# Sliding-window attention beside a dense layer: block 0's queries from raw x, exponentials summed by halving adds, and a new order of the pieces

## The chip, the cores and the metric

The kernel runs on one core of a Trainium2 chip. The metric is the device time of one execution in microseconds (us). The engines run side by side and meet by semaphores: TensorE (PE: matrix products, with its weight loads PEld), VectorE (DVE), ScalarE (ACT), GpSimd (POOL) and SyncE (SP), which issues most of the DMA transfers. The median of the three runs shown is 209.95 us (209.86 to 210.22).

## The reference

x has 2048 rows of 640 in bf16. It is normalized row by row; the normalized rows go through two layers side by side, and both results are added to x:

```python
xn = layernorm(x)                       # (x - mean) / sqrt(var + 1e-5)
# A: 32 heads of 20; each row looks at itself and at 7 rows, 2 apart, before it
q, k, v = split(xn @ wqkv)
logits = einsum("bhsd,bhswd->bhsw", q, kg) * 20 ** -0.5   # kg: the 8 rows of k
attn = softmax(where(mask, logits, -1e9))
A = einsum("bhsw,bhswd->bhsd", attn, vg) @ wo
# B: dense, 1536 wide
B = gelu(xn @ w1 + b1) @ w2 + b2
out = x + A + B
```

## The kernel before, in words

**Tiles.** The rows come in four chunks (n = 0 to 3) of 512, each of four blocks of 128. A normalized block is turned, so that the 640 columns lie on partitions in five tiles of 128 (xnT). Chunk 0's blocks are turned by TensorE (do_tp, L274) and copied out of PSUM (do_tc, L282); the other chunks by DMA (do_td, L290). From xnT come q, k and v (do_pj, L331, evicted by do_pc, L397) and the dense layer's hidden tiles (do_f1, L595, with the gelu in do_ge, L607). VectorE multiplies q by the shifted k (do_qk, L428), adds some of the five column tiles (do_pa L461, do_pb L467), and TensorE sums over each head (do_lg, L472). Then comes the softmax over eight positions (do_max, do_sub, do_exp, do_sum, do_recip, do_attn, L507 to L549), the weights are spread over the partitions by DMA (expand, L560), VectorE multiplies them by v and adds (do_av L575, do_add L585, do_ot L589) to oT, and TensorE forms the result from the hidden tiles and oT: turned for chunks 0 to 2 (do_t, L663, the DMAs do_ut and do_ud), straight for chunk 3 (do_o, L620).

**Order.** Nothing is scheduled by the compiler: ORDER (L41 to L71) lists some 700 pieces by name, and each engine runs its instructions in the order in which the pieces are listed. A name tells the piece, the chunk and the part: `f10_5` is do_f1 of chunk 0 and tile 5, `lg2` is do_lg of chunk 2, `t004` is the part of do_t for chunk 0 and column tile 0 that multiplies oT. An instruction that must wait holds back all that is listed behind it on its engine. The same holds for SP's transfers. PSUM has four buffers for products (psA), two for turned blocks and results (psO) and one for scores (psL).

**The start.** SP loads block 0 of x, ScalarE's queue block 1; then SP loads q's weights in one transfer, k's, blocks 2 and 3, v's, and so on (L134 to L146). TensorE runs 13 products of ones (do_warm, L443) so that it is not idle at first. Block 0's mean and variance come from VectorE (do_st, L206), block 1's from ScalarE by sums (do_su L220, do_sq L227, do_mean1 L236). do_rs (L241) makes the reciprocal deviation, do_xn (L259) normalizes, and q of blocks 0 and 1 is formed 128 columns at a time as xnT grows (do_ga, do_gd, L347 to L373). From then on, chunk 0's q, k and v are formed for two blocks at once (do_gp, L375, evicted by do_gq, L388).

**The sums.** do_sum (L528) adds the eight exponentials of each head and row in one reduction on VectorE, read with the positions innermost, into a small f32 tile. do_recip (L534) takes its logarithm and exponential on ScalarE. Chunk 0's softmax runs in two halves (PARTS, L34).

Of the kernel before, what the change touches and what calls it, by code (L numbers as in the profile page):

```python
# [32 lines left out]
TURNED = 4  # L33
PARTS = (2, 1, 1, 1)  # L34
# [7 lines left out]
pad01 pad02 st00a st00 sum1 rs00 mean1 neg1 sq1 xn00a xn00b tp00a wa tp00b wb tc00a tc00b rs01 ga xn01a xn01b gb2  # L42
tp01a gb3 tp01b tc01a tc01b gb4 gd gc0 ge tb b1 hj102 gc1 ho st02a st02 st03a hc102 gc4 st03 hj101 rs02 xn02 rs03 xn03
st10a st12a st13a st11a hc101 st12 hj100 hc100 hj200 tp02 tc02 tp03 tc03 pk st13 hj201 hc200 st11 st10 hj202 hc202
hj012 hc012 hc201 rs1 rc1 hj112 hc112 xn12 tc12 xn10 hj210 qk000 hj011 hc011 tc10 hj110 hc110 qk001 hj010 hc010 hc210
hj111 hc111 qk011 qk010 pa011 pa001 xn11 tc11 xn13 hj211 hc211 f10_5 tc13 f10_4 ge0_4 ge0_5 f10_0 ge0_0 f10_7 f10_10
pj113 pc113 pj103 pj111 ge0_10 pj101 pc111 pj114 ldx ge0_7 pa000 pc101 pa010 lg0 mask m0a ld2 pc103 pj102 pc114 pad11
su21 mx0a ex0a pj112 pc112 m0b mx0b ss0a pc102 ex0b ri0a ss0b pj100 pc100 at0a ri0b at0b pj110 pj104 pc104 pc110 xd0
qk111 f10_2 ge0_2 su22 qk100 hj212 hc212 f10_6 ge0_6 pj121 su20 f10_1 pc121 su23 ldo f11_10 ge1_10 ng2 ge0_1 sq20
f11_5 f10_11 pj122 pc122 f10_3 qk110 sq22 t040 qk101 f11_0 t000 lg1 xp0 av010 ge0_3 sq21 xs0 ge1_0 sq23 rs2 f10_8  # L50
ge0_8 t001 m1 f11_3 rc2 xn23 tc23 ge0_11 av031 t041 mx1 av021 xn20 tc20 f11_7 av011 ge1_5 ge1_7 av001 ge1_3 xp1 f10_9
t042 t002 xn21 ge0_9 tc21 pj120 xn22 tc22 av030 av000 f11_9 ge1_9 pj124 ex1 av020 ss1 pc120 pc124 pj123 pc123 ad00 ri1
t043 f11_2 t003 pj204 at1 pc204 xd1 su31 ad01 pad12 ad02 ot0 pj200 pc200 pj201 pc201 av101 xp2 pj212 su30 pc212 pj220
pj213 pc220 pc213 pj223 pc223 pj211 su33 pc211 pj203 su32 ng3 sq33 pad21 av100 sq31 pj202 f11_6 t004 u00 av110 xs1
av130 t044 av120 av131 av121 t010 av111 t011 t012 t013 u04 t020 t014 sq32 pc203 pc202 pj221 sq30 rs3 rc3 ad11 u01 ut00
ad10 ad12 t030 pj210 pc221 t031 t021 t022 ut01 ge1_2 pj214 xn33 tc33 t032 t033 t034 xn31 tc31 ge1_6 pj224 t023 t024
f11_8 ot1 pc214 pad22 pc210 qk201 qk211 qk210 xn30 tc30 f12_9 qk200 f11_1 pa210 pa201 xn32 ge1_8 u02 pa211 pa200 f11_4
ge1_1 t100 ge1_4 tc32 pj311 pc311 pb212 ud00 ud01 ge2_9 pj310 pc310 pad31 pj304 pc304 pj314 pc314 t101 pj300 pj324
pc324 ut02 pj303 f12_10 pb202 pc224 u03 pc303 xp3 pj301 pc301 xl ge2_10 pc300 f13_9 pj313 pc313 pj312 ud02 ut03 ud03
pj302 pc302 f13_6 ge3_6 pj323 lg2 pc312 qk300 m2 pc323 f11_11 ge1_11 f13_0 ge3_0 mx2 ut04 f13_11 ge3_9 ex2 pa300 ss2  # L60
qk310 ri2 at2 xs2 qk301 t130 t131 f12_1 ge2_1 ge3_11 t132 f13_10 qk311 t102 t103 f13_2 pa310 xd2 t104 pj320 pc320
f13_1 ge3_1 u10 ut10 ud10 f12_8 pa311 pa301 pb312 ge2_8 f13_8 ge3_8 t110 t133 t111 t112 t113 t114 u11 ge3_10 f12_5
pj222 pc222 pj321 pc321 pb302 lg3 av200 t134 u13 m3 av221 ge2_5 xb3 f12_11 t140 t141 t120 ut11 mx3 f12_2 ge3_2 av211
ex3 ss3 ri3 av220 ge2_2 f13_5 ge2_11 t142 t143 t121 t122 t123 f12_6 ge2_6 at3 xs3 f12_3 ge2_3 t124 u12 f12_7 pj322
ud04 av210 av201 av231 f12_0 t144 ge2_7 ge2_0 t200 av230 pc322 u14 ut12 ud11 f12_4 ge2_4 ge3_5 f13_4 ge3_4 o310 f13_7
ge3_7 t210 ad20 ad21 ad22 ot2 f13_3 t201 t202 pad32 av321 t203 ge3_3 o311 av331 ut13 av320 xd3 t204 u20 av300 ut14
ut20 ud12 ud13 t211 t212 t240 t213 t214 av311 u21 ud20 t241 t242 av310 av330 t220 t221 t222 t223 t224 u22 ut21 t243
av301 ad30 ad31 o330 o331 t230 ad32 t231 t232 t233 t234 u23 ut22 ud21 t244 u24 o312 ut23 o313 ud22 ud23 ot3 o320 o321
o322 o323 o324 oc32 od32 ut24 o314 oc31 od31 o300 o301 o302 o303 o304 o332 o333 o334 ud14 ohi ud24 oc30 od30 oclo ochi
ochd  # L70
# [4 lines left out]
def kernel(  # L75
# [63 lines left out]
    load_w(0)  # L139
    load_w(1)  # L140
    load_x(2, BPC)
    load_w(2)
# [21 lines left out]
    make_identity(nc, ident[:])  # L164
    eps_t = consts.tile([P, 1], F32, name="eps_t")
# [70 lines left out]
    def do_mean1():  # L236
        nc.vector.tensor_scalar(
            out=mv[:, 1, 0:1], in0=col(acc, 0, 1), scalar1=1.0 / D, scalar2=None, op0=ALU.mult
        )

    def do_rs(n, b0, b1):  # L241
        sl = slice(n * BPC + b0, n * BPC + b1)
        summed = n in ACT_STATS or (n, b0) == (0, 1)
        table(LOG_SET)
        nc.scalar.activation(
            logv[:, sl], mv[:, sl, 1], ACT.Ln, bias=eps_t[:], scale=1.0 / D if summed else 1.0
        )
        nc.scalar.activation(rstd[:, sl], logv[:, sl], ACT.Exp, scale=-0.5)
# [95 lines left out]
    def bank(key):  # L344
        return get(("bank", key), lambda: psA.tile([P, BPC, P], F32, tag="acc", name="gps"))

    def q_piece(bl, to, ti, first, last):  # L347
        ps, slot = (bank(bl), to) if to < BPC else (bank(BPC), bl)
        nc.tensor.matmul(  # L349
            ps[:, slot, :],  # L350
            lhsT=wqkv_p[0][:, ti, to, :],
            rhs=tiles["xnT", 0][:, ti, bl * P : (bl + 1) * P],
            start=first,
            stop=last,
            skip_group_check=True,
        )

    def do_ga(a, b):
        for ti in range(a, b):
            for to in range(KT):  # L360
                q_piece(0, to, ti, ti == 0 and to in (0, BPC), ti == KT - 1 and to == BPC - 1)

    def do_gd(a, b):
        for ti in range(a, b):
            for to in range(KT):
                q_piece(1, to, ti, ti == 0 and to == 0, ti == KT - 1 and to >= BPC - 1)

    def do_gc(g):
        q = pair_of(0, 0)
        if g == BPC:  # L370
            nc.scalar.copy(q[:, BPC, 0 : 2 * P].rearrange("p (b m) -> p b m", b=2), bank(BPC)[:, 0:2, :])
        else:
            nc.scalar.copy(q[:, 0:BPC, g * P : (g + 1) * P], bank(g)[:])  # L373

    def do_gp(which, pair, a, b):  # L375
        ps = psA.tile([P, 2, 2 * P], F32, tag="acc", name="gps")
        tiles["pair", which, pair, a] = ps
        for to in range(a, b):
            for ti in range(KT):
                nc.tensor.matmul(  # L380
                    ps[:, to - a, :],
                    lhsT=wqkv_p[which][:, ti, to, :],
                    rhs=tiles["xnT", 0][:, ti, pair * 2 * P : (pair + 1) * 2 * P],
                    start=(ti == 0),
                    stop=(ti == KT - 1),
                )
# [112 lines left out]

    def shifted(n, i):  # L500
        cs, width = part(n, i)
        if PARTS[n] == 1:
            return tiles["L", n][:]
        low = half[0][:].rearrange("p w t c -> p (w t c)").bitcast(F32)[:, 0 : W * P]
        return low.rearrange("p (i w c) -> p i w c", i=PARTS[n], w=W)[:, i, :, :]

# [21 lines left out]
    def do_sum(n, i):  # L528
        total = softmax_tile("sums", n, [P], F32)
        nc.vector.tensor_reduce(  # L530
            out=total[:, i, :], in_=tiles["e", n][:, i, :, :].rearrange("p w c -> p c w"), axis=AX.X, op=ALU.add
        )

    def do_recip(n, i):  # L534
        rs = get(("rs", n), lambda: smp.tile([P, PARTS[n], P // PARTS[n]], F32, tag="m", name="rs"))
        total = tiles["sums", n][:, i, :]
# [4 lines left out]
    def do_attn(n, i):  # L541
        cs, width = part(n, i)
        attn = get(("attn", n), lambda: smp.tile([P, W, P], BF16, tag="attn", name="attn"))
# [171 lines left out]
    for name in "tb b1 mean1 ho ldx ld2 ldo xl oclo ohi ochi ochd mask pk".split():  # L715
        piece(name, locals()[f"do_{name}"])
    for u, a, b, eng in (("a", 0, 2, "ve"), ("b", 2, KT, "se")):
        for bl in range(2):
            piece(f"xn0{bl}{u}", do_xn, 0, bl, a, b)
            piece(f"tp0{bl}{u}", do_tp, 0, bl, a, b, True)  # L720
        piece(f"tc00{u}", do_tc, 0, 0, a, b, "ve")
        piece(f"tc01{u}", do_tc, 0, 1, a, b, eng)
    for bl in range(BPC):
        if bl != 1:
            piece(f"st0{bl}a", do_st, 0, bl, 0)
            piece(f"st0{bl}", do_st, 0, bl, 1)
        piece(f"rs0{bl}", do_rs, 0, bl, bl + 1)
        if bl > 1:
# [3 lines left out]
    piece("sum1", do_su, 0, 1)  # L732
    piece("neg1", do_ng, 0, 1, 2)
    piece("wa", do_warm, 1, P)
    piece("wb", do_warm, 2, P)
    piece("sq1", do_sq, 0, 1)
    piece("ga", do_ga, 0, 2)
    for ti in range(2, KT):
        piece(f"gb{ti}", do_ga, ti, ti + 1)
    piece("gd", do_gd, 0, 2)  # L740
    piece("ge", do_gd, 2, KT)
    for g in (0, 1, BPC):
        piece(f"gc{g}", do_gc, g)
    for which in range(3):
        for pair in range(0 if which else 1, 2):
            for g, (a, b) in enumerate(COLS):
                piece(f"hj{which}{pair}{g}", do_gp, which, pair, a, b)
# [100 lines left out]
```

## Time and profile before

| | |
|---|---|
| median of the runs | 209.95 us (209.86 to 210.22) |
| the profiled execution | 210.03 us, of which the profile's span is 208.0 us |
| TensorE busy | 203.5 us, 1164 products |
| VectorE busy | 180.9 us, 141 instructions |
| ScalarE busy | 127.5 us, 234 instructions |
| first product with real data | 5.46 us (a turn of block 0) |
| first product of q | 6.25 us |
| first product of k | 9.53 us |
| VectorE's first product of q and k | 17.77 us |
| oT of chunks 0, 1, 2, 3 done | 81.8, 103.1, 172.5, 193.8 us |
| TensorE's last product done | 204.8 us |

The page gives busy times and 40 slices of the span; the timeline gives single instructions with their start, their duration and, in brackets, how long the engine was idle before and what ended the wait. A matrix product's duration covers its way through the array, and the next one starts before it ends; so TensorE's rate is read from the distance between two starts.

### The profile page before, as it was taken

To read this page: it belongs to the slowest core of one execution; us is meant where nothing else is said; L and a number is where in the kernel's file an instruction comes from. 1 tells how busy PE (TensorE), PEld (TensorE's weight loads), DVE (VectorE), ACT (ScalarE), POOL (GpSimd) and SP (SyncE) were. 2 spreads that over 40 slices of the span, in tenths; PEclk is the share of its full clock that TensorE was granted. 3 is DMA by queue.
4 is the path that set the end of the run, shared out by engine and by line. 5 is a ranking of instruction groups with operands and counts; after the bars stand their busy time and mean duration, and the time that the engine had idled before them with its cause. 6 is when DMAs were issued, how large, how long until landed. Compare 5 with 4: busy or idle time off the path is not lost.

```text
span 208.0 us, 2951 instructions
## 1 busy us (share of the span) xinstructions
PE 203.5 (98%) x1164; PEld 107.0 (51%) x1164; DVE 180.9 (87%) x141; ACT 127.5 (61%) x234; POOL 24.9 (12%) x37
## 2 busy tenths in 40 slices
PE   8999999999999999999999999999999999999993
PEld 3999754554445554444455544444444444445552
DVE  2598995999699999999999989999999999999201
ACT  5589968898997877877564556744658541112210
POOL 2000000000000000220020610002200402222621
PEclk9999999999999999999999999999999999999999
DMA  6994379168426075148431790086405795556753
GB/s 217 388 395 137 68 207 395 60 122 238 162 82 162 11 189 138 25 50 91 90 25 56 114 123 0 0 188 81 37 0 100 121 108 54 50 50 76 49 68 63
DMA packets 36863, 23.88 MB, mean 115 GB/s; under 512 B 24946, under 2 KB 34674, under 8 KB 36850
## 3 DMA queue, kind: packets, MB, share of 16 engines
q1 hardware_dynamic: 26320, 18.75, 34.5%
q0 software_dynamic: 8752, 2.95, 17.8%
q10 hardware_dynamic: 1778, 2.00, 2.7%
q8 instruction: 9, 0.15, 0.3%
q14 instruction: 4, 0.03, 0.0%
HBM read 10.00 MB, written 5.57 MB: 75 GB/s over the span
## 4 chain that ended last, share of the span: by engine, by line
PE 66%; DVE 21%; ACT 9%; DMA 2%; issue 1%; DVEq 0%; ACTq 0%
PE T L673 17%; PE pps L336 15%; PE hps L599 13%; PE lo L634 7%; PE gps L380 7%; DVE half L433 5%; DVE half L587 4%; DVE sums L530 3%; PE idle L446 2%; ACT L173 2%; DVE half L465 2%; DMA xnT<-xn 2%; DVE half L578 2%; ACT hT L615 2%; PE hi L636 2%; PE gps L349 1%
## 5 line engine op out<-in xcount | busy, mean ns | idle before, releaser
L599 PE MATMUL hps<-xnT,w_sb 128*128 128x512 bf16 x240 | 56.9, 379 | 0.1
L433 DVE TENSOR_TENSOR half<-qT,kT 128x5120 bf16<-128x5120 bf16 x16 | 44.3, 2820 | 1.0 <-ACT vT L400 0.7
L673 PE MATMUL T<-hT,w_sb 128*128 128x512 bf16 x180 | 43.3, 379 | 0.0
L685 POOL DMA_DIRECT2D out_dram<-x_sb x15 | 19.5, 1357 | 172.8 <-DMA x_sb<-x_sb 168.7
L599 PEld LDWEIGHTS <-w_sb 128*128 128x128 bf16 x240 | 23.3, 98 | 28.2 <-issue 1.2
L615 ACT ACTIVATE hT<-hps,bT 128x512 bf16<-128x512 f32 x36 | 24.1, 687 | 7.3 <-PE hps L599 7.2
L673 PEld LDWEIGHTS <-w_sb 128*128 128x128 bf16 x180 | 17.6, 98 | 21.1
L578 DVE TENSOR_TENSOR half<-vT,ax 128x2560 bf16<-128x2560 bf16 x16 | 23.1, 1484 | 2.4 <-PE L L479 2.4
L676 ACT ACTIVATE x_sb<-T,bT 128x512 bf16<-128x512 f32 x15 | 10.3, 687 | 23.6 <-PE T L673 23.6
L578 DVE TENSOR_TENSOR half<-vT,x_sb 128x2560 bf16<-128x2560 bf16 x16 | 22.6, 1485 | 0.0
L587 DVE TENSOR_TENSOR half<-half,half 128x5120 bf16<-128x5120 bf16 x8 | 22.3, 2820 | 0.1
L673 PE MATMUL T<-oT,wo 128*128 128x512 bf16 x75 | 18.3, 379 | 0.3 <-DVE oT L592 0.3
L336 PE MATMUL pps<-xnT,wk_sb 128*128 128x512 bf16 x75 | 18.3, 379 | 0.0
L336 PE MATMUL pps<-xnT,wv_sb 128*128 128x512 bf16 x75 | 18.3, 379 | 0.0
L336 PE MATMUL pps<-xnT,wq_sb 128*128 128x512 bf16 x75 | 18.2, 379 | 0.0
L173 ACT ACT_TABLE_LOAD x12 | 15.4, 1283 | 0.9 <-PEq L832 0.7
L465 DVE TENSOR_TENSOR half<-half 128x2048 bf16<-128x2048 bf16 x12 | 13.9, 1217 | 0.0
L336 PEld LDWEIGHTS <-wv_sb 128*128 128x128 bf16 x75 | 8.8, 117 | 7.6
L336 PEld LDWEIGHTS <-wq_sb 128*128 128x128 bf16 x75 | 8.7, 118 | 7.7 <-issue 0.4
L336 PEld LDWEIGHTS <-wk_sb 128*128 128x128 bf16 x75 | 8.8, 117 | 7.5
L263 ACT ACTIVATE xn<-x_sb,nmr,rstd 128x640 bf16<-128x640 bf16 x12 | 10.6, 916 | 3.2 <-DMA xnT<-xn 2.3
L400 ACT CAST vT<-pps 128x512 bf16<-128x512 f32 x15 | 8.5, 589 | 6.1 <-PE pps L336 6.1
(92 smaller groups left out, 241.0 us busy)
## 6 DMA issues: line engine op xcount, KB each, us to landing
w_sb<-in_B_w_dram SPq DMA_DIRECT2D x4, 960.0 KB, 10.3
ax<-attn SPq DMA_DIRECT2D x8, 256.0 KB, 4.8
x_sb<-attn SPq DMA_DIRECT2D x8, 256.0 KB, 4.6
out_dram<-x_sb POOLq DMA_DIRECT2D x15, 128.0 KB, 4.0
x_sb<-in_A_x_dram SPq DMA_DIRECT2D x1, 1280.0 KB, 6.5
out_dram<-x_sb ACTq DMA_DIRECT2D x2, 640.0 KB, 3.1
wq_sb<-in_A_wqkv_dram SPq DMA_DIRECT2D x1, 800.0 KB, 4.7
wk_sb<-in_A_wqkv_dram SPq DMA_DIRECT2D x1, 800.0 KB, 6.3
```

The lines of the kernel that those rows point to most:

```text
L173: nc.scalar.preload_act_table_set(name)
L336: nc.tensor.matmul(ps[:], lhsT=wqkv_p[which][:, ti, to, :], rhs=xnT[:, ti, :], start=(ti == 0), stop=(ti == KT - 1),)
L380: nc.tensor.matmul(ps[:, to - a, :], lhsT=wqkv_p[which][:, ti, to, :], rhs=tiles["xnT", 0][:, ti, pair * 2 * P : (pair + 1) * 2 * P], star ...
L433: nc.vector.tensor_tensor(out=half[h][:, :, :, cs], in0=q[:, :, at].unsqueeze(1).to_broadcast([P, W // 2, KT, 2 * P]), in1=window(k, h, at ...
L465: nc.vector.tensor_tensor(out=even, in0=even, in1=odd, op=ALU.add)
L578: nc.vector.tensor_tensor(out=half[h][:, :, :, cs], in0=window(qkv_tile(n, 2), h, cs), in1=ax_view(n)[:, j, ws, :].unsqueeze(2).to_broadca ...
L587: nc.vector.tensor_tensor(out=a, in0=a, in1=b, op=ALU.add)
L599: nc.tensor.matmul(ps[:], lhsT=w1_sb[:, ti, ft * P : (ft + 1) * P], rhs=tiles["xnT", n][:, ti, :], start=(ti == 0), stop=(ti == KT - 1),)
L615: nc.scalar.activation(hT, tiles["hps", n, ft][:], ACT.Gelu_apprx_tanh, bias=bT[:, ft : ft + 1], scale=1.0)
L634: nc.tensor.matmul(lo[:], lhsT=lhs, rhs=rhs[:, 0:CH], start=first, stop=last)
L673: nc.tensor.matmul(ps[:], lhsT=lhs, rhs=rhs, start=pc == 0 and k == 0, stop=pc == 4 and k == len(srcs) - 1)
L685: nc.gpsimd.dma_start(dst, src, accum_op=ALU.add)
```

## The change

- **Block 0's q from raw x.** Five turns of raw x (`tr`) are copied by ScalarE (`cra`, `crb`), with a column of ones beside them, and multiplied by q's weights (`ra0` to `ra4`); the 129th column then holds the sums of the weights. When mean and deviation are known, two f32 products with the identity (`fa0`, `fa1`) spread the reciprocal deviation and minus mean times it over all partitions; ScalarE copies them and the weight sums (`cf`, `ws0`, `ws1`), and VectorE multiplies the raw result by the one (`ev0`, `ev1`) and adds the product of the others (`eq0` to `eq4`). Block 0 is still normalized and turned for k, v and the dense layer. q of block 1 is formed as before, but after block 0's.
- **Loads.** q's weights come in five transfers, one for each tile of rows, k's in two; x of blocks 2 and 3 goes ahead of k's. k of the first two blocks is formed in two steps accordingly (`hj10gp` and `hj10g`).
- **Statistics of block 1** come from VectorE, as those of block 0; its sums on ScalarE and do_mean1 go.
- **Sums.** do_sum adds the halves: four positions to four, two to two, one to one, in f32. In chunk 0 into a free part of a product buffer, in the other chunks into the tile that later holds the weights.
- **ORDER** is another order of all pieces, down to the last chunk.

```diff
-    load_w(0)
-    load_w(1)
+    for ti in range(KT):
+        nc.sync.dma_start(wqkv[0][:, ti, :], wqkv_v[:, ti, 0:D])
     load_x(2, BPC)
+    for ts in (slice(0, KEARLY), slice(KEARLY, KT)):
+        nc.sync.dma_start(wqkv[1][:, ts, :], wqkv_v[:, ts, D : 2 * D])
...
+    def do_tr():
+        tp = psO.tile([P, 2 * CH], BF16, tag="o", name="tp")
+        tiles["tr"] = tp
+        for t in range(KT):
+            nc.tensor.transpose(tp[:, t * P : (t + 1) * P], x_sb[:, 0, t * P : (t + 1) * P], ident[:])
+
+    def do_cr(a, b):
+        nc.scalar.copy(x_raw[:, a:b, 0:P], tiles["tr"][:, a * P : b * P].rearrange("p (t m) -> p t m", t=b - a))
+
+    def do_ra(ti):
+        for g, (a, b) in enumerate(RAW):
+            for to in range(a, b):
+                nc.tensor.matmul(
+                    raw_ps(g)[:, to - a, 0 : P + 1],
+                    lhsT=wqkv_p[0][:, ti, to, :],
+                    rhs=x_raw[:, ti, 0 : P + 1],
...
+    def do_fa(f):
         nc.tensor.matmul(
+            lead_ps()[:, f, :],
+            lhsT=(rstd, nmr)[f][:, 0:1].to_broadcast([P, P]),
+            rhs=ident32[:],
...
+    def do_ev(g):
+        a, b = RAW[g]
+        nc.vector.tensor_tensor(
+            out=scaled[:, a:b, :],
+            in0=raw_ps(g)[:, 0 : b - a, 0:P],
+            in1=factors[:, 0, :].unsqueeze(1).to_broadcast([P, b - a, P]),
+            op=ALU.mult,
+        )
+
+    def do_eq(to):
+        nc.vector.scalar_tensor_tensor(
+            out=pair_of(0, 0)[:, to, 0:P],
+            in0=factors[:, 1, :],
+            scalar=w_sums[:, to : to + 1],
+            in1=scaled[:, to, :],
+            op0=ALU.mult,
+            op1=ALU.add,
+        )
...
     def do_sum(n, i):
-        total = softmax_tile("sums", n, [P], F32)
-        nc.vector.tensor_reduce(
-            out=total[:, i, :], in_=tiles["e", n][:, i, :, :].rearrange("p w c -> p c w"), axis=AX.X, op=ALU.add
-        )
+        a, e = sums(n, i), tiles["e", n][:, i, :, :]
+        nc.vector.tensor_tensor(out=a, in0=e[:, 0 : W // 2, :], in1=e[:, W // 2 :, :], op=ALU.add)
+        for k in (2, 1):
+            nc.vector.tensor_tensor(out=a[:, 0:k, :], in0=a[:, 0:k, :], in1=a[:, k : 2 * k, :], op=ALU.add)
```

The order's beginning, before and after, to k's first products:

```diff
-pad01 pad02 st00a st00 sum1 rs00 mean1 neg1 sq1 xn00a xn00b tp00a wa tp00b wb tc00a tc00b rs01 ga xn01a xn01b gb2
-tp01a gb3 tp01b tc01a tc01b gb4 gd gc0 ge tb b1 hj102 gc1 ho st02a st02 st03a hc102 gc4 st03 hj101 rs02 xn02 rs03 xn03
+pad01 pad02 tr st00a wa cra st01a crb st01 rs01 ra0 ra1 wb st00 rs00 xn01a xn01b ra2 ra3 tp01a tp01b tc01b xn00 fa0 ho
+nm0 tc01a st03a ra4 tp00 tc00 gd st03 rs03 st02a ge st02 gc0 fa1 cf xn03 ws0 ev0 gc1 eq1 hj101p rs02 xn02 ws1 ev1 eq3
```

## The prediction

> **What bounds the kernel now.** I read the page's first part, then the busy digits, then the waits, and last the timelines of the places where something waits.
>
> ```profile
> span 208.0 us, 2951 instructions
> PE 203.5 (98%) x1164; PEld 107.0 (51%) x1164; DVE 180.9 (87%) x141; ACT 127.5 (61%) x234; POOL 24.9 (12%) x37
> ...
> PE   8999999999999999999999999999999999999993
> ...
> DVE  2598995999699999999999989999999999999201
> ```
>
> TensorE (PE) is busy in every slice; VectorE (DVE) has room only in the first slices and the last three. "Busy" counts pipelined products, so I also took the spacing of the products' starts: 0.216 us for 512 columns all the way (five products of line 599 fill 1.08 us of the chain of waits). Larger spacings, after the start, are few. Two of the three largest, in the timelines:
>
> ```profile
> 80.31 1.49 DVE L592 TENSOR_TENSOR oT<-half 128x2560 bf16<-128x2560 bf16 x1
> ...
> 81.21 0.10 PEld L673 LDWEIGHTS <-wo 128*128 128x128 bf16 x1
> ...
> 81.86 1.46 PE L673 MATMUL T<-oT,wo 128*128 128x512 bf16 x6 [0.28 <-DVE oT L592]
> ```
>
> ```profile
> 145.22 1.05 PE L479 MATMUL L<-half,head_of 128*32 128x512 bf16 x16 [0.17 <-DVE half L470]
> ```
>
> By starts, 0.44 us is lost at 81.86 (VectorE's oT came late), 0.24 at 145.22 (VectorE's partial sums), and 0.25 at 157 (ScalarE, ACT, was behind with the gelu). That is 0.93 us that a better order can win inside. The rest is the start, up to 6.25 us, and the tail after the last product (204.8 to 208.0), which the change leaves alone. So the time is TensorE's start, plus its work, plus about one microsecond.
>
> **The start.**
>
> ```profile
> 4.57 0.95 PE L446 MATMUL idle<-const-bfloat16-1.0 128*128 128x512 bf16 x4
> 5.46 0.39 PE L280 MATMUL tp<-ident,xn 128*128 128x128 bf16 x2
> ...
> 6.25 1.00 PE L349 MATMUL gps<-xnT,wq_sb 128*128 128x128 bf16 x15
> ...
> 9.53 0.30 PE L380 MATMUL gps<-xnT,wk_sb 128*128 128x256 bf16 x1
> ```
>
> ```profile
> 5.89 0.78 DVE L285 COPY xnT<-tp 128x256 bf16<-128x256 bf16 x2 [0.20 <-PE tp L280]
> ```
>
> The 13 warm-up products hold TensorE until 5.31 us (the last is issued at 5.21). They and the turns up to 6.1 stand 0.107 us apart for 128 columns; from 6.2 on it is 0.056. So the clock doubles there. q's weights landed at 5.86 and the first normalized x at 6.17, so the weights were not what block 0 waited for.
>
> **The change part by part.**
>
> *Raw x first.* The five turns (tr) may go at 5.31 instead of 5.46. But both copies (cra, crb) wait for the fifth turn: in the new order crb has no wait of its own. The fifth is issued at 5.31 + 4 x 0.107 = 5.74 and lands 0.31 later, at 6.05. cra copies 256 columns on ScalarE: between 0.29 (VectorE's 256-column copy) and 0.48 (ScalarE's 384-column copy); I take 0.37, ScalarE's 256-column cast from PSUM. With 0.04 and 0.07 for two hand-overs (5.84 to 5.88 and 6.17 to 6.24 in the rows), the first raw product starts at 6.53: **+0.28** against 6.25.
>
> *TensorE's work up to k's projections.* Before, 6.25 to 9.53 holds 50 products of 128 columns (2.80), block 1's five turns (0.28) and tb (0.20). After: 25 raw products of 129 columns (1.41), two warm-ups that now run inside the stage (0.11), block 1's turns (0.28), 25 products of block 1 (1.40), block 0's turns of normalized x (0.28; k and v still need them, so tr comes on top), and the two fp32 products fa0, fa1 that spread deviation and mean. No row shows an fp32 product: from 0.056 (bf16, 128 columns) to 0.38 (the longest duration of any product's row); I take 0.30 each, **0.60**, near 0.216, the spacing of a product of four times the columns, with a weight load (0.1) in the open. [...] tp01b: rs01 and rs00 now queue on ScalarE behind cra and crb, so rstd of block 1 comes at about 7.28, xn01b ends at 7.95, and TensorE, done with ra3 at 7.76 and the first two turns at 7.88, waits **0.13**. Sum after: 1.41 + 0.11 + 0.28 + 1.40 + 0.28 + 0.60 + 0.13 = 4.21, and tb (0.20) follows later; 4.41 against 3.28 is +1.13. With the start, TensorE is **1.41 us later** for everything behind.
>
> *The five loads.* They bring nothing to the sum: at 6.53 all but perhaps the last chunk have landed (one load of the same bytes landed at 5.86). SP issues four DMAs more at about 0.45 each, and each further one waits on an earlier landing; x of blocks 2 and 3 moves ahead of k's weights. Those landed at 7.98; 320 KB at the 0.39 MB/us of the first windows is 0.8 more, 8.8, while k's first product is now at 10.7: hidden by 1.9, and lost only beyond that. Below nothing: x 2 and 3 come up to 2 us earlier (8.81 before), but their turns stand behind k on TensorE.
>
> *The corrections* (ev 2x, eq 5x, nm0, block 1's statistics) go to VectorE, cf, ws, cra, crb and tc00 to ScalarE, for sum1, sq1 and three copies. eq is about 0.2 each, ev 0.46 and 0.33 (f32 at the 1.1 ns an element of line 516). Behind them on VectorE stand chunk 1's statistics (4.1 us from 12.99 to 17.09) and rs1's round trip (0.6). ev0 waits for cf and ws0 on ScalarE, behind gc0, at 11.7, the eqs end near 13.8, so the first product of q and k starts near 18.7 instead of 17.77: +0.9. Who waits for that? The scores lg0; VectorE's eight instructions (4 x 2.74 + 4 x 1.13) then end at 34.2, but TensorE comes to lg0 only at about 35.8. Hidden.
>
> *Sums by halving.*
>
> ```profile
> L530 DVE TENSOR_REDUCE sums<-e 128x128 f32<-128x1024 bf16 x3 | 5.8, 1917 | 0.3 <-ACT e L526 0.3
> L530 DVE TENSOR_REDUCE sums<-e 128x64 f32<-128x512 bf16 x2 | 2.1, 1057 | 0.0
> L516 DVE TENSOR_TENSOR half<-L,m 128x512 f32<-128x512 f32 x2 | 1.4, 692 | 0.1
> ```
>
> Three dependent adds of 512, 256 and 128 elements: 0.69 (line 516's f32 row), then 0.42 and 0.29 by taking 1.04 ns an element off it, and 0.07 between: 1.47 against 1.9. That is 0.43 less in each of chunks 1 to 3, and nothing in chunk 0 (0.69/2-sized pieces come to 1.0, as now). Between 0 (all three at 0.69: no gain) and 0.8 less (no latency). As TensorE is the bound, this pays only where TensorE waits for VectorE: at 81.86 and 145.22.
>
> *The new order.* I added the rows' durations up to each meeting point. TensorE comes to the first product with oT of chunk 0 near 83.8, with VectorE ready at 83.1 (it is held by lg1, which TensorE brings 2.2 later); to lg2 at about 122, VectorE 122.0; lg3 145.8 on both; chunk 2's oT 173.4 against 172.8; chunk 3's 194.3 against 194.1. So TensorE's delay closes the old waits (-0.93), and with margins that thin I put 0.2 for new ones. xp0's transfer (x of chunk 0 to the output) moves behind chunk 2's turned loads on SP, to about 67; such a transfer lands in 3.1, so it is done before at1 (near 76) lets the expansions overwrite its source.
>
> **Sum:** 1.41 - 0.93 + 0.20 = +0.68. The profiled execution took 210.03 us for its span of 208.0; 210.71, less the 0.08 by which that lies above the median of 209.95, is **210.6 us**: slower by 0.3%. A difference under 0.2% (0.42 us) can hardly be told from none.
>
> **Rivals.**
>
> *Cheap fp32 products: no slower.* If fa0 and fa1 cost 0.056 each like a bf16 product, the sum is 0.68 - 0.49 = +0.19, 210.1 us. It decides from a joint price under 0.34. For it: the program has one instruction for each. Against: nothing cheaper than bf16's spacing is in any row, and four-byte weights can hardly load faster than the 0.1 of two-byte ones. If the new waits stay out too, 209.9. Chance 0.27 for this and all that ends near it.
>
> *The old waits live on.* VectorE waits for TensorE's scores (2.29 us at the mask, 1.69 after lg1), so it is late by the same 1.4 us, and the three meetings are as tight as before. Then nothing is won back: 1.41, and 0.2: 211.6 us. For it: the margins above are 0 to 0.7 us. Against: the halved sums give VectorE 0.43 in a chunk, and its queue has 0.6 us less of sums and no new work after 18 us. Chance 0.23.
>
> *A late clock.* TensorE now stands idle from 5.96 to 6.53, across 6.18 where the clock doubled. If the doubling has to be earned anew, in the 5.4 us that it took from the first warm-up at 0.78, TensorE runs at half speed that long and loses 2.7: 213.3. [...] Against: 0.57 us idle of several. Chance 0.05.
>
> *It doesn't do what it says*: the products wait for the copy, not for weights, whichever order the loads have; that is in the forecast already.
>
> **Chances.** Forecast (210.3 to 211.1) 0.45, cheap products 0.27, old waits 0.23, late clock 0.05. The lowest corner that I can price is the cheap case with a copy of 0.29 (-0.08), no wait at tp01b (-0.13) and no new waits: 1.41 - 0.49 - 0.93 - 0.21 = -0.22, 209.7. Faster by over 0.2% (under 209.53) takes a gain beside these: 0.09, out of the cheap case. Within 0.2% (to 210.37): the rest of that case (0.18) and 0.11 from the forecast's low side, 0.29. Slower: 0.62. The range takes in all but the late clock and the unpriced gain, with 0.4 above the old waits' 211.6 for fp32 products of more than 0.30 each: 209.6 to 212.0.
>
> **What would show it.** The first raw product at 6.5 and k's first at 10.7; each fa product at 0.3; L530's successors at 1.47 for a chunk; the wait before T<-oT at 82 and before lg3 gone; the last product near 205.3. It is wrong if raw products start before 6.3, if TensorE's spacing beyond 10 us shows waits of over half a microsecond, or if the clock doubles after 6.6.

## The result, and the profile after

The changed kernel takes 212.16 us (median; 211.40 to 212.50) against 209.91 for the kernel before: a ratio of 1.0099 [1.0070, 1.0129], slower by about 2.2 us. Measured again on another chip the ratio was 1.0073 [1.0061, 1.0085], 1.6 us. The forecast was 210.6, slower by 0.3%, with a range up to 212.0. The direction is right; the size is a third of what came, and the time lies 0.16 us above the range.

The profiled execution is the quickest of its four: 211.40 us, for a span of 209.0, 1.37 over the one profiled before. The page's first part:

```profile
span 209.0 us, 3001 instructions
PE 204.3 (98%) x1173; PEld 107.8 (52%) x1173; DVE 181.2 (87%) x158; ACT 126.0 (60%) x234; POOL 25.1 (12%) x39
```

As before, TensorE is busy throughout. A 98% in both kernels tells nothing of the 1.3 us between them; only distances between starts do. In the PE timeline's start (start, us, line, tile):

```profile
5.31 0.74 PE L366 MATMUL tp<-ident,x_sb 128*128 128x128 bf16 x5
...
6.61 0.74 PE L374 MATMUL raw<-lead,wq_sb 128*128 128x129 bf16 x10 [0.45 <-ACT lead L369]
...
8.18 0.44 PE L389 MATMUL lead_ps<-ident,rstd 128*128 128x128 f32 x2
8.46 0.45 PE L374 MATMUL raw<-lead,wq_sb 128*128 128x129 bf16 x5
...
10.41 0.44 PE L389 MATMUL lead_ps<-ident,nmr 128*128 128x128 f32 x2
10.69 2.89 PE L453 MATMUL gps<-xnT,wk_sb 128*128 128x256 bf16 x25
```

The first raw product starts at 6.61 (forecast 6.53), released by the copy cra, and k's first at 10.69 (10.74). Each fa product shows as two records and takes 0.28 from its start to the next product's (8.18 to 8.46, 10.41 to 10.69; forecast 0.30). So the start and TensorE's added work came out nearly as worked out: k's first product is 1.16 later and tb's 0.19 comes behind it, **+1.35** against +1.41.

The old waits have gone. By starts, nothing stands open at the first product with chunk 0's oT, at the scores of chunk 3, or near 157:

```profile
82.21 1.49 DVE L676 TENSOR_TENSOR oT<-half 128x2560 bf16<-128x2560 bf16 x1
...
84.71 1.24 PE L757 MATMUL T<-oT,wo 128*128 128x512 bf16 x5
```

```profile
145.58 1.24 PE L757 MATMUL T<-oT,wo 128*128 128x512 bf16 x5
146.75 1.05 PE L553 MATMUL L<-half,head_of 128*32 128x512 bf16 x16
```

oT is ready 1 us before its first product now, and lg3 follows five products of 0.216 (1.08) at once. **-0.93**, as forecast. But two waits are new, 0.71 at 30.14 and 0.13 at 73.92: **+0.84**, where the forecast put 0.20. The sum 1.35 - 0.93 + 0.84 = 1.26 accounts for the end: VectorE's last addition starts at 206.13 instead of 204.84, 1.29 later.

**The wait at 30 us** in the timelines of three engines:

```profile
19.82 0.16 DVE L256 SCALAR_TENSOR_TENSOR nmr<-mv,rstd 128x4 f32<-128x4 f32 x1 [0.88 <-ACT rstd L249]
19.90 2.82 DVE L507 TENSOR_TENSOR half<-qT,kT 128x5120 bf16<-128x5120 bf16 x1
```

```profile
18.77 0.59 ACT L469 CAST kT<-gps 128x512 bf16<-128x512 f32 x1 [0.36 <-PE gps L453]
19.25 0.30 ACT L246 ACTIVATE logv<-mv,eps_t 128x4 f32<-128x4 f32 x1
...
20.02 0.92 ACT L264 ACTIVATE xn<-x_sb,nmr,rstd 128x640 bf16<-128x640 bf16 x1
...
26.70 0.92 ACT L264 ACTIVATE xn<-x_sb,nmr,rstd 128x640 bf16<-128x640 bf16 x1 [0.80 <-DMA xnT<-xn]
...
28.11 1.28 ACT L179 ACT_TABLE_LOAD   x1
29.40 1.85 ACT L699 ACTIVATE hT<-hps,bT 128x512 bf16<-128x512 f32 x3
```

```profile
30.14 1.02 PE L683 MATMUL hps<-xnT,w_sb 128*128 128x512 bf16 x4 [0.55 <-ACT hT L699]
```

Read it upward. TensorE has filled its four product buffers and waits for the first gelu. The gelu waits for ScalarE's table load at 28.11, and that stands behind the fourth normalization of chunk 1, which waits for a transfer that turns an earlier normalized block. The first normalization starts at 20.02 instead of 17.89 before: VectorE ends chunk 1's statistics at 18.90 instead of 17.10, and the reciprocal deviations (L246) then queue 0.3 behind a cast of k that waits for TensorE. The table load is 3.08 later than before (25.03), TensorE only 1.35. TensorE pays part of the difference.

Of these 3.08, 0.80 is the fourth normalization's wait for that transfer, more than the 0.71 that TensorE loses. The transfer is the second of chunk 1's four, issued at 22.37. It signals its landing sixteen times; fifteen signals came by 24.74, the sixteenth at 26.68, while the other three transfers have all of theirs within 0.2. At 24.32 a packet of 16 KB on the queue that the profile names *instruction* began, and took 1.27. In the six profiled executions in which such a packet began just before this transfer's signals (the changed kernel, e1, e2, e8, e9, e10), one signal came 1.5 to 2 us after the others, and TensorE waited near 30 us, by 0.21 to 0.74; in the other eight the signals came together, and it did not wait there (seven of these have the old start and order, e7 the old start alone). That the packet held up the one signal is an inference: the trace doesn't tell which transfer engine carried it.

**The loads** (rows of the DMA view, 2 to 10 us, before and after; 40 slices of 0.2 us):

```profile
GB/s 147 307 333 320 320 295 277 346 393 367 393 390 410 397 397 397 384 326 365 394 390 379 385 384 390 397 391 403 384 397 384 397 397 397 397 384 403 390 397 410
DMA packets 2425, 2.96 MB, mean 370 GB/s; under 512 B 114, under 2 KB 2425, under 8 KB 2425
```

```profile
GB/s 218 205 218 327 371 371 373 337 346 326 196 141 166 160 211 327 339 327 295 288 307 320 333 371 282 198 250 250 301 352 352 358 327 358 365 346 359 333 339 320
DMA packets 2057, 2.39 MB, mean 299 GB/s; under 512 B 192, under 2 KB 2057, under 8 KB 2057
```

The stream sags to 141 to 211 GB/s from 4.0 to 5.0 us and stays lower: k's first weights land at 10.18 (forecast 8.8, before 7.98), v's at 13.13 (before 10.84), and VectorE waits for chunk 1's x until 14.79.

### The profile page after: what moved, and what is told of

The parts are those of the page before. It is cut to its first block, busy times and chain, and to the rows that moved or that the text cites. A ratio compares the mean times of both kernels' runs of the same rounds, so it can differ in the third digit from the quotient of the medians.

```text
span 209.0 us, 3001 instructions
## 1 busy us (share of the span) xinstructions
PE 204.3 (98%) x1173; PEld 107.8 (52%) x1173; DVE 181.2 (87%) x158; ACT 126.0 (60%) x234; POOL 25.1 (12%) x39
## 4 chain that ended last, share of the span: by engine, by line
PE 93%; ACT 3%; DMA 2%; issue 0%; DVE 0%
PE T L757 26%; PE pps L337 23%; PE hps L683 23%; PE lo L718 7%; PE gps L453 3%; PE L L553 3%; PE idle L520 2%; DMA xnT<-xn 2%; PE hi L720 2%; ACT xn L264 1%; PE raw L374 1%; ACT L179 1%; PE tp L281 1%; ACT kT L469 1%; PE gps L432 1%; ACT vT L469 0%
## 5 line engine op out<-in xcount | busy, mean ns | idle before, releaser
L683 PE MATMUL hps<-xnT,w_sb 128*128 128x512 bf16 x240 | 56.2, 379 | 0.5 <-ACT hT L699 0.5
L769 POOL DMA_DIRECT2D out_dram<-x_sb x15 | 20.0, 1343 | 172.5 <-DMA x_sb<-x_sb 172.3
L474 ACT CAST qT<-pps 128x512 bf16<-128x512 f32 x15 | 8.5, 591 | 6.3 <-PE pps L337 6.3
```

The costliest lines, as they stand in the source:

```text
L683: nc.tensor.matmul(ps[:], lhsT=w1_sb[:, ti, ft * P : (ft + 1) * P], rhs=tiles["xnT", n][:, ti, :], start=(ti == 0), stop=(ti == KT - 1),)
L769: nc.gpsimd.dma_start(dst, src, accum_op=ALU.add)
```

## The experiments

Times are medians; each ratio is to the kernel before on the same chip, with its 95% interval. Two things were to be told apart: where the 1.3 to 2.2 us come from (loads, start, order), and whether the halving adds do anything for it.

**e1, the changed kernel again, and e2, q's weights in one load.**

```diff
-    for ti in range(KT):
-        nc.sync.dma_start(wqkv[0][:, ti, :], wqkv_v[:, ti, 0:D])
+    load_w(0)
```

> The changed kernel once more, to see how far its executions lie apart (211.4 to 212.5 in the first four) and to have a second profile. Theory L (loads): q's weights in five loads slow the stream of transfers in the first 10 us, v's weights and x of chunk 1 land some 2 us late, by an amount that differs from one execution to the next; this profile then shows other landing times than the first, and its time moves with the wait of TensorE near 30 us (0.71 us in the first). Theory W (work): the time above before is TensorE's added work and its later start; then the time is within 0.2 us of the first whatever the landings, and the spread has another place. Both: 211.4 to 212.5.

> The changed kernel with q's weights in one load again, all else as it is. Theory L: the last of q's weights land near 5.9 instead of 7.1, x of chunk 1 near 12.9 instead of 14.7, VectorE's first product of q and k starts near 18.9 instead of 19.9, the wait of TensorE near 30 us (0.71) falls below 0.2, and the executions lie closer together: 210.6 to 211.2. Theory W: the wait near 30 comes from ScalarE's order and stays, the start is the same: 211.8 to 212.3.

e1: 211.58, 1.0073 [1.0061, 1.0085]. e2: 211.22, 1.0048 [1.0032, 1.0064]. In e1's profile k's weights are late for TensorE itself, which the forecast had hidden by 1.9:

```profile
10.45 1.72 PE L453 MATMUL gps<-xnT,wk_sb 128*128 128x256 bf16 x14 [0.51 <-DMA wk_sb<-in_A_wqkv_dram]
```

By starts that is 0.68; beside it stand 0.74 at 29.96 and 0.81 at 72.26. In e2 the stream is back near 390 GB/s and k is not waited for, yet 0.40 at 29.49 and 0.54 at 71.52 stay. The two intervals just overlap: one load brings some 0.4 us, and most of the loss remains.

**e3, the kernel before with five loads alone, and e4, with the halving sums alone.**

```diff
-    load_w(0)
+    for ti in range(KT):
+        nc.sync.dma_start(wqkv[0][:, ti, :], wqkv_v[:, ti, 0:D])
```

```diff
-        nc.vector.tensor_reduce(
-            out=total[:, i, :], in_=tiles["e", n][:, i, :, :].rearrange("p w c -> p c w"), axis=AX.X, op=ALU.add
-        )
+        nc.vector.tensor_tensor(out=a, in0=e[:, 0 : W // 2, :], in1=e[:, W // 2 :, :], op=ALU.add)
+        for k in (2, 1):
+            nc.vector.tensor_tensor(out=a[:, 0:k, :], in0=a[:, 0:k, :], in1=a[:, k : 2 * k, :], op=ALU.add)
```

> The kernel before with q's weights in five loads, in its own order, k's in one load behind them and x of blocks 2 and 3 behind k's, all else as before. Theory L: the last chunk lands near 7.1, so TensorE waits some tenths for it in q of block 0, and all that lands later is 1 to 2 us late; x of chunk 1 near 14, VectorE's first product of q and k near 19: 210.5 to 211.5. Theory W: the loads are hidden in this kernel too: 209.8 to 210.1.

> The kernel before with the sums by halving adds alone. By the prediction's step a chunk's sum takes 1.47 us instead of 1.9 in chunks 1 to 3 and the same in chunk 0, and it pays where TensorE waits for VectorE, at 81.9 (0.44) and 145.2 (0.24): 209.3 to 209.6. Rival: VectorE's time is not what TensorE waits for there, or the small adds cost as much as the reduction: 209.8 to 210.1.

e3: 211.52, 1.0072 [1.0056, 1.0088]: five loads cost the old kernel 1.5 us. Its PE timeline:

```profile
10.36 2.92 PE L381 MATMUL gps<-xnT,wk_sb 128*128 128x256 bf16 x25 [0.84 <-DMA wk_sb<-in_A_wqkv_dram]
13.75 1.29 PE L381 MATMUL gps<-xnT,wv_sb 128*128 128x256 bf16 x10 [0.46 <-DMA wv_sb<-in_A_wqkv_dram]
...
23.66 1.25 PE L381 MATMUL gps<-xnT,wk_sb 128*128 128x256 bf16 x10 [0.92 <-ACT qT L396]
```

TensorE waits for k, then for v, then for a ScalarE that is late by then (by starts 0.91, 0.63 and 1.08, together 2.62). The profiled execution is e3's longest, 212.31, so these waits are at the upper end.

e4: **209.10**, 0.9956 [0.9944, 0.9968], faster than both kernels. The adds take 0.69 + 0.43 + 0.29 = 1.41 us in a chunk, against 1.92 for the reduction:

```profile
L614 DVE TENSOR_TENSOR attn<-e 128x512 f32<-128x512 bf16 x3 | 2.1, 688 | 0.0
...
L616 DVE TENSOR_TENSOR attn<-attn 128x256 f32<-128x256 f32 x3 | 1.3, 425 | 0.1
L616 DVE TENSOR_TENSOR attn<-attn 128x128 f32<-128x128 f32 x3 | 0.9, 292 | 0.1
```

(These are the changed kernel's groups; the shapes are the same.) In e4's timeline VectorE's oT ends before TensorE comes to it, and lg3 follows five products at once:

```profile
79.66 1.49 DVE L602 TENSOR_TENSOR oT<-half 128x2560 bf16<-128x2560 bf16 x1
...
81.27 1.89 PE L683 MATMUL T<-oT,wo 128*128 128x512 bf16 x8
```

So the three old waits were worth what the forecast said (0.93), and the adds alone win all of it; the third, at 157, is gone too, which e4's expectation had not counted.

**e5, the kernel before with q in two loads, and e6, five loads with the bias loads moved to GpSimd's queue.** e6 asks why small loads slow the stream: in e3, k's load was issued only at 4.11, since it waited for an earlier landing. The changed kernel's trace shows such waits: its first eight transfers signal eight semaphores, and the ones behind them take these again. SP issued the ninth at 3.25, the first one's landing being complete at 3.23, the tenth at 4.05 (the second's at 4.04) and the eleventh at 5.09 (the third's at 5.08).

```diff
-    load_w(0)
+    for ts in (slice(0, 3), slice(3, KT)):
+        nc.sync.dma_start(wqkv[0][:, ts, :], wqkv_v[:, ts, 0:D])
```

```diff
-    nc.scalar.dma_start(b_rt[0:FT, :], B_b1.rearrange("(t p) -> t p", p=P))
-    nc.scalar.dma_start(b_rt[FT : FT + KT, :], B_b2.rearrange("(t p) -> t p", p=P))
-    load_w(0)
+    nc.gpsimd.dma_start(b_rt[0:FT, :], B_b1.rearrange("(t p) -> t p", p=P))
+    nc.gpsimd.dma_start(b_rt[FT : FT + KT, :], B_b2.rearrange("(t p) -> t p", p=P))
+    for ti in range(KT):
+        nc.sync.dma_start(wqkv[0][:, ti, :], wqkv_v[:, ti, 0:D])
```

> The kernel before with q's weights in two loads (three tiles and two), all else as before: one load more instead of four. With five, k's weights landed at 10.3 instead of 8.0 and the time was 1.5 us more. Theory S (slots): there are eight completion slots for the loads; the ninth load waits until an earlier one has landed, so with five loads k's are issued at 4.1 instead of 1.7, few loads are under way and the transfer engines run dry. With two loads k's still need no slot that is taken, so they land by 8.3 and the time is that of before: 209.8 to 210.3. Theory P (price of a load): each small load costs the stream some half a microsecond by itself; k's land at 8.5 or later and the time is 210.3 to 210.6.

> The kernel before with q's weights in five loads, and the two small loads of the biases on GpSimd's queue instead of ScalarE's, which frees two of the eight completion slots; k's weights then wait for no slot. Theory S: k's are issued near 3.7, the stream keeps near 390 GB/s, they land by 8.6, and the time falls from 211.5 to 209.9 to 210.5. Theory P: the stream is as slow as with five loads before, k's land at 9.5 or later, 211 to 211.6.

e5: 209.95, 0.9988 [0.9958, 1.0018], no difference; its profile is of one of two late executions (211.02) and shows the second load late by 0.9 at 8.16. e6: 211.51, 1.0048 [1.0016, 1.0080]. k's load is issued at 3.65 without a wait, and the rate falls all the same, to 128 to 186 GB/s between 4.4 and 5.0:

```profile
GB/s 339 378 352 320 275 362 283 298 323 246 251 250 179 128 186 262 237 224 275 307 326 301 346 352 339 320 371 339 384 320 352 365 346 352 352 333 371 390 326 339
```

So the wait for a landing isn't the cause. What is left is the small loads themselves; by what they slow the stream, no run shows.

**e7, the old start and the halving sums, with the new order from chunk 1's statistics on; e8, the new start (q in one load) and the halving sums, with the old order.** Both join the two lists at a splice that belongs to neither kernel.

```diff
 ORDER = """
-(the pieces behind the start)
+(the other kernel's pieces behind the start)
```

> The kernel before (one load for q, normalized queries) with the sums by halving and with the changed kernel's order from the statistics of chunk 1 on; the old start up to there. It tells the new order from the new start, beside the same sums in the old order (209.1). Theory O (the new order itself is worse: its waits of TensorE near 29 and 71 us, 0.4 and 0.3 in the changed kernel with one load, come from its places on ScalarE): 209.5 to 210.0, with these waits in the profile. Theory B (the new start brings them, by being a microsecond late on VectorE and ScalarE): 208.8 to 209.2, without them.

> The changed kernel with q's weights in one load and with the order of before from tb on; the new start, the halving sums. Beside the old start in the same order (209.1) it gives the price of raw queries alone. By the prediction's step the new start puts TensorE 1.41 us later: with the trace's two fp32 products (0.28 each instead of 0.30) 1.35, so 210.4 to 210.7 if nothing behind gives it back or adds to it. Theory B (a late VectorE and ScalarE add waits further on in any order): 210.8 to 211.4. Where the old order has slack for VectorE and TensorE is the bound alone, the 1.35 stands.

e7: 210.36, 1.0001 [0.9976, 1.0027]; 1.3 above e4, of which 0.84 is a wait at the splice (turns at 13.23), so the new order is worth nothing or less with the old start. TensorE does not wait near 30 us, although ScalarE is as late as in e2 (first normalization at 19.61; e2: 19.67) and TensorE is ready for the place at the same time (29.04; 29.09). The fourth normalizations and the table loads, e2 first:

```profile
26.05 0.92 ACT L263 ACTIVATE xn<-x_sb,nmr,rstd 128x640 bf16<-128x640 bf16 x1 [0.49 <-DMA xnT<-xn]
...
27.46 1.28 ACT L178 ACT_TABLE_LOAD   x1
```

```profile
24.57 1.74 ACT L262 ACTIVATE xn<-x_sb,nmr,rstd 128x640 bf16<-128x640 bf16 x2
...
26.80 1.28 ACT L172 ACT_TABLE_LOAD   x1
```

In e2 the second transfer's last signal came at 26.02, 1.6 after the others; in e7 all sixteen were in by 24.38, and the instruction packet began at 24.43. e8: 211.99, 1.0081 [1.0057, 1.0105]; 2.9 above e4. Its profiled execution is the quickest of twelve (211.21): there the last product starts 1.97 later than in e4's profile, of which 1.01 is a wait at the splice (tb at 11.04), 0.75 the start, and 0.21 a wait at 29.36, in the old order. What the slower executions add, no profile shows. Both are weak, because of the splices, but neither shows a gain of the change beside the sums.

**e9, the changed kernel with the old reduction.**

```diff
-        nc.vector.tensor_tensor(out=a, in0=e[:, 0 : W // 2, :], in1=e[:, W // 2 :, :], op=ALU.add)
-        for k in (2, 1):
-            nc.vector.tensor_tensor(out=a[:, 0:k, :], in0=a[:, 0:k, :], in1=a[:, k : 2 * k, :], op=ALU.add)
+        nc.vector.tensor_reduce(
+            out=total[:, i, :], in_=tiles["e", n][:, i, :, :].rearrange("p w c -> p c w"), axis=AX.X, op=ALU.add
+        )
```

> The changed kernel, but the eight exponentials summed by one reduction as before (the rest, five loads and new order too, stays). Theory (the halving adds win by closing TensorE's waits for VectorE, as in the kernel before, where they alone won 0.9 us): with 1.92 us instead of 1.41 per chunk VectorE is about 0.5 later at each oT, so TensorE waits again at the first product with oT and before the scores of chunk 3: 212.2 to 212.9, 0.4 to 1 us over the changed kernel's 211.6 to 212.2. Rival (TensorE is late by itself in the new order, so VectorE has slack): no wait over 0.2 us beyond 75 us and the changed kernel's time within 0.3 us.

e9: 212.45, 1.0100 [1.0073, 1.0127]. Its profile has the wait for VectorE again:

```profile
148.02 1.05 PE L553 MATMUL L<-half,head_of 128*32 128x512 bf16 x16 [0.21 <-DVE half L544]
```

That is 0.28 by starts beyond the step of 0.09 that such a place has without a wait (as at 146.75 in the changed kernel); there is 0.18 at 159.76, and none at oT. At 74.91 there is 0.59 (0.13 at the same product in the changed kernel): ScalarE waits 1.25 for the sums before it takes their logarithm, and then frees a product buffer late. Together that is 0.9 more than in the changed kernel, in the expected size, though partly in another place. The ratio's interval covers both of the changed kernel's ratios, so the time alone doesn't show it.

**e10, the changed kernel with the old list of loads.** This one puts the loads' theory to the test.

```diff
-    for ti in range(KT):
-        nc.sync.dma_start(wqkv[0][:, ti, :], wqkv_v[:, ti, 0:D])
-    load_x(2, BPC)
-    for ts in (slice(0, KEARLY), slice(KEARLY, KT)):
-        nc.sync.dma_start(wqkv[1][:, ts, :], wqkv_v[:, ts, D : 2 * D])
+    load_w(0)
+    load_w(1)
+    load_x(2, BPC)
```

> The changed kernel with the list of loads of the kernel before: q's weights in one load, k's in one, x of blocks 2 and 3 behind them. Theory (the small loads are what the forecast left out): the stream runs at about 390 GB/s, k's weights land near 8.0 us, x of chunk 1 near 12.5, VectorE's first product of q and k starts near 18.9 instead of 19.9, TensorE's wait near 30 us is under 0.3; time 210.3 to 211.0, near the forecast that counted the loads at nothing (210.7 by span). Rival (the new order and the new start are late by themselves): the waits near 30 and 72 us stay as with q in one load alone (0.41 and 0.32), 211.2 or more.

e10: 212.18 (211.28 to 213.07), 1.0106 [1.0072, 1.0140]. **The theory falls.** The stream is as before (365 GB/s in the mean, k's weights at 8.17, chunk 1's x at 12.75), and still VectorE's first product of q and k starts at 19.81 and TensorE waits:

```profile
19.73 0.16 DVE L254 SCALAR_TENSOR_TENSOR nmr<-mv,rstd 128x4 f32<-128x4 f32 x1 [1.29 <-ACT rstd L247]
19.81 2.82 DVE L505 TENSOR_TENSOR half<-qT,kT 128x5120 bf16<-128x5120 bf16 x1
```

```profile
29.93 1.24 PE L681 MATMUL hps<-xnT,w_sb 128*128 128x512 bf16 x5 [0.42 <-ACT hT L697]
...
72.04 1.25 PE L335 MATMUL pps<-xnT,wk_sb 128*128 128x512 bf16 x5 [0.46 <-DMA xnT<-xn]
```

With x early, VectorE only waits longer for the reciprocal deviation (1.29 instead of 0.88), which ScalarE still makes in its place in the order. By starts there are 0.28 at 11.26, 0.58 at 29.93 and 0.62 at 72.04: 1.48 of new waits. Its account closes too: 10.32 for k's first product is 0.79 later, tb 0.20, so 0.99 - 0.93 + 1.48 = 1.54; the last product starts 1.56 later than before. The start is 0.36 shorter than in the changed kernel's profile because the five turns ran faster (the clock doubled at 5.15 instead of 6.23), and the order's waits take it back.

**e11, the kernel before with q in five loads from two queues.**

```diff
+    for ti in range(KT):
+        (nc.scalar if ti % 2 else nc.sync).dma_start(wqkv[0][:, ti, :], wqkv_v[:, ti, 0:D])
     nc.scalar.dma_start(b_rt[0:FT, :], B_b1.rearrange("(t p) -> t p", p=P))
...
-    load_w(0)
```

> The kernel before with q's weights in five loads, of which the second and the fourth are issued from ScalarE's queue instead of SyncE's. Theory A (short loads leave one queue empty between them, as each must be issued and fetched by itself): with two queues side by side the rate stays near 390 GB/s from 4 to 9 us, the last chunk lands by 6.3, k's weights by 8.3, and the time is within 0.4 us of before (209.7 to 210.4). Theory B (each small load costs the engines a fixed time, wherever it is issued): the rate falls under 300 GB/s between 4 and 6 us as with one queue, k's weights land after 9.5, and the time is 211.2 to 211.8.

e11: 211.87, 1.0090 [1.0056, 1.0125]. It doesn't decide. The rate holds better (321 GB/s over 2 to 10 us, lowest slice after 3 us 218, against 279 and 141 in e3), but k still lands at 10.11, and the edit disturbed something else: ScalarE's first issue put its table load off from 0.74 to 4.14, so that block 0 was normalized late and TensorE stood idle before the first turn:

```profile
7.12 0.39 PE L281 MATMUL tp<-ident,xn 128*128 128x128 bf16 x2 [1.60 <-DVE xn L266]
```

The clock doubled at 9.92 there, and fifteen products took 1.81 instead of 1.00.

**e12, e4 again on another chip.**

> The kernel before with nothing changed but the sums (halving adds), once more on this chip: 209.0 to 209.4 against before's 209.9 to 210.1, ratio 0.994 to 0.998, and TensorE's waits near 82, 145 and 157 us gone. If the first such measurement was a chance of its chip, the ratio's interval takes in 1.

e12: 209.12, 0.9952 [0.9938, 0.9966]. The gain of the sums alone stands on two chips; of all that was run, it is the quickest version.

## Why the prediction was right, and where it was wrong

| step of the prediction | forecast | measured |
|---|---|---|
| start and work up to k and tb | +1.41 | +1.35 |
| first raw product; each fp32 product | 6.53; 0.30 | 6.61; 0.28 |
| old waits closed | -0.93 | -0.93 |
| new waits | +0.20 | +0.84 (e1: 2.2, e10: 1.48) |
| k's weights; margin to their product | 8.8; 1.9 | 10.18; 0.5 (e1: -0.68) |
| VectorE's first product of q and k | 18.7 | 19.90 |
| halving adds, a chunk | 1.47 | 1.41 |
| oT of chunks 0, 2, 3 | 83.1, 172.8, 194.1 | 83.7, 173.5, 194.8 |

**Right.** It is slower for the reason given: TensorE is the bound, its start and its added work come to 1.4 us, and the waits that a better order could close are only 0.93. The first raw product of that profile was released by the copy, not by weights. The rival of cheap fp32 products is refuted: at 0.28 a piece, 0.56 for the two, they cost nearly what was put (0.60). The old waits did not live on. The clock doubled at 6.23, not late.

That the start agrees so well is in part luck. Its two terms missed in opposite ways: the first raw product came 0.36 later (forecast 0.28), and the work from there to k took 4.08 (4.21; the wait at tp01b came to about 0.04, not 0.13). And the turns' speed hangs on when the clock doubles (in the profiles of both kernels, products of 128 columns start 0.107 us apart before it and 0.056 after). It did so at 6.2 in the profiles of both kernels; in e1 it doubled at 4.01, the first raw product started at 5.69, and k's first could have started at 9.77, only 0.24 later than before. That execution was no quicker: the time went into the waits.

**Wrong: "with margins that thin I put 0.2 for new ones".** The new waits came to 0.84 in the profiled execution and more in others; 0.71 of it in one place, which the forecast itself had named as a sign of being wrong. Two steps behind that term failed.

The first is "Who waits for that? ... Hidden." The step followed VectorE's lateness (19.9, even 1.2 later than forecast) to the scores and found it covered, and that was true: nothing near 36 us waits. It did not follow ScalarE, where the four normalizations of chunk 1 and the gelu's table load stand behind the same reciprocal deviation, nor the transfers of the turned blocks, for which the fourth normalization waits. There the lateness grew from 2.1 us at the first normalization to 3.1 at the table load, 0.80 of it by the one late signal, and came out at 30 us as a wait of TensorE's. e2 and e10, with q's load and with all loads as before, keep the wait, and e8, with the old order, has 0.21 of it; e7, as late as e2 but without the late signal, has none. So lateness alone did not make it. Near 72 us it is chunk 2's turned blocks: in e1, e2 and e10 the last such transfer, issued at 67.4 to 67.9, landed 3.9 to 4.2 later, an instruction packet of 1.3 to 1.7 us having begun at 68.4 to 69.0, and TensorE waited 0.54 to 0.81; in the changed kernel's profile, e7 and e9 that packet came after 71, the transfer landed in 2.4, and nothing waited for it. What these packets bring, and why they come then, no run shows.

The second is "The five loads. They bring nothing to the sum." The rate was taken from one large load and used for five small ones. Alone, five loads cost the old kernel 1.5 us (e3). In the changed kernel they eat the margin at k's weights, and sometimes more (0.68 in e1). But they do not add up with the rest: the same lateness is paid once, by the loads or by the order. Their share in the changed kernel is between nothing (e10) and 0.4 (e2), and these two runs, on different chips, don't settle it. Why executions of the changed kernel spread from 211.4 to 212.5 stays open as well; e1 and e9 suggest k's weights (0.68 at 10.45, 0.82 at 11.39) and e1 the wait near 72, but of the changed kernel itself no execution above 211.81 was profiled.

**A rival that wasn't priced** is the change's own good part. The forecast booked the -0.93 to the order, the adds and the delay together. e4 shows that the adds alone bring it (in e9, without them, TensorE's delay closes the one at oT, but not the others). The new start and the new order, which make up most of the change, cost 2.5 to 3 us on top (211.58 and 212.16 against 209.10).

## What to carry to other kernels

Where one engine is the bound, price a change by that engine's start, its added work and its list of waits, and try each part alone: here three adds in place of a reduction won all there was to win. When a step becomes late, follow every engine that has something queued behind it, not only the one that seemed critical. If a wait ends with a transfer, see what else the transfer engines did at that moment. And don't price several small loads by the rate of a large one.

## What the runs showed of the hardware

- **Small loads slowed the whole stream.** 160 KB at a time instead of 800 took the mean over 2 to 10 us from 370 to 279 GB/s (e3), with 65 ns in the mean for a packet on SP's queue from 3.5 to 6 us, mostly of 1280 bytes, instead of 55, and with idle time on the engines (share 0.83 from 4 to 5 us). A wait for landings isn't the reason: in e6 k's load was issued without one, and the rate fell to 128 GB/s all the same. The traces show more packets of four bytes on that queue (61 against 16 from 3.5 to 6 us in e3); what they are, and whether they slow the stream, no run shows.
- **A transfer was as late as its last signal.** Of the sixteen signals of one turned block's transfer, one came 1.5 to 2 us after the rest in six profiled executions, each time beside a 16 KB instruction packet of 1.0 to 1.3 us. In the changed kernel's profile that signal came at 26.68, the other fifteen by 24.74, and the normalization that waited for the transfer started at 26.70. That the two shared a transfer engine is not shown.
- **The moment of the clock's doubling varied.** TensorE was busy with the same warm-up from 0.78 us in every run, and the clock doubled between 3.69 (e12) and 6.23 us, and at 9.92 in e11, 2.8 us after 1.6 us of idleness. What sets the moment, no run shows. e11 fits the late-clock rival, though with 2.8 us where the rival put 5.4; in the changed kernel (0.45 us idle), e2 (0.78) and e12 (0.83) idleness put nothing off or back.
